# A gated linear attention with a maxout layer: tiles of 128 tokens of one sequence become tiles of 64 tokens of two sequences

## The chip, the cores and the metric

The kernel runs on one core of one Trainium2 chip. The metric is the device time of one execution in microseconds (us). Before the change it is 564.7 us, the median of three runs from 564.04 to 565.69 us.

## What is computed

There are four sequences of 768 tokens and eight heads of 48. Each head keeps a complex 48x48 state that is turned and damped at each token by a gate, takes in an outer product of key and value, and is read by the query. The result, 3072 rows of 384, goes through a maxout layer.

```python
# q, k, v, a_re, a_im: (4, 8, 768, 48); w1, w2, w3: (384, 768); w_out: (768, 384)
mag = np.sqrt(a_re * a_re + a_im * a_im)
scale = np.minimum(mag, 0.999) / (mag + 1e-06)
a_re_n, a_im_n = a_re * scale, a_im * scale
for t in range(768):                       # S_re, S_im start at 0, per batch and head
    new_re = ar * S_re - ai * S_im         # ar, ai: gate of token t, one per row of the state
    new_im = ar * S_im + ai * S_re
    S_re, S_im = new_re + outer(k[t], v[t]), new_im
    y[t] = q[t] @ S_re
x = y.transpose(0, 2, 1, 3).reshape(3072, 384)
out = maximum(maximum(x @ w1, x @ w2), x @ w3) @ w_out
```

## The kernel before

**Tiles and groups.** A tile is 128 tokens of one sequence, that is two chunks of 64, on the 128 partitions. A group is two tiles, called x and y, of two different sequences. There are 12 groups: groups 0 to 5 walk through sequences 0 and 1, groups 6 to 11 through sequences 2 and 3. So the recurrence runs through six groups, and group 6 starts again from an empty state. Inside a tile chunk 1 needs the state that chunk 0 leaves.

**From gates to scores.** For a group, `gates` (L502) works out the logarithm of the gate's size (`Ln`) and its angle in turns (`w`) from `ar` and `ai`. In the word `cs` of `angles` (L583) TensorE sums the angles over the tokens by products with the triangular matrix `upto`: for chunk `ch` of the tile, `lhsT` is all 128 rows of `upto` by the 64 columns of that chunk, so chunk 1 gets the sum over the whole tile. There are four such products per tile (two chunks, even and odd heads), each of 192 columns; a product of 32-bit floats shows as two instructions in the trace. Words `t` (ScalarE) and `nf` (VectorE) take the sum to its fraction of a turn. Word `Cd` (L598) carries it on: two GpSimd-issued DMAs per tile add the last row of `nf` to row 0 of the next group's `ar`, where word `turn` (VectorE) picks it up before the next `cs`. In the last group of a sequence there is no `Cd`. `turns` (L619) sums `Ln` in the same way in the word `sums`, but over chunks of 64 alone, as products of 64 rows by 64 columns in four quarters of the array (eight products per tile). Keys and queries are scaled and turned (`mk`, `mq`, `uk`, `uq`), transposed (`tpk`, `tpq`), weighted by blocks (`factors`, L684: `Q1`, `Q2`, `KB`, `QB`, `QG`), and give the scores `A` and `B`, which VectorE picks into `atm` by masks (`g0` to `g3`).

**State.** `state` (L767): word `kEn` weights the keys, `dk` is the outer products of keys and values for both chunks (four heads only in a sequence's last group), and the words `h0` to `h3` take the state on: `h0`/`h1` decay it and add `dk` of chunk 0, `h2`/`h3` the same for chunk 1, each on 112 partitions by 384 elements on VectorE (the very first `h1` is a copy on ScalarE). Word `y` of `outputs` (L802) adds the scores times the values and the state times the weighted queries `QG`; chunk 0 of a sequence's first tile has no state, so `QG` is made for half of the heads' columns there.

**The layer.** The features of a group are 384 x 256. From `w2 - w1` and `w3 - w1` it takes `U01, U02, U11, U12` products, with the maximum on ScalarE or VectorE (`u..`); `w1` with `w_out` is one product made at the start. The last product is done by seven block products (`P1` to `P7`, sums `S1` to `S4`, joins `r..`, `ox`, `oy`). Group 0 uses plain products instead. The weights come in 12 blocks (`WL0` to `WL11`) whose bits VectorE and ScalarE rearrange at the start (`Wa` to `Wg`).

**Order.** `SCHEDULE` (L21) lists 1903 words, `name` + tile + group (`csx:3`); class `Bound` (L200) makes every engine issue its instructions in that order. `SLOTS` (L125) names the PSUM room for each use, and `OTHER` (L132) the words that go to the second engine they can run on: loads to GpSimd's queue instead of SyncE's (SP), copies and absolute values to VectorE instead of ScalarE, `addw` and `Lnop` to VectorE instead of an adding DMA of GpSimd. Loads (L367 to L392): `Lr`, `Li` bring 128 rows of `a_re`, `a_im` in one transfer; `Lk`, `Lq`, `Lv` take four transfers of 64 rows and four heads each. `D` (L946) writes 128 rows of the result.

Of the kernel before, what the change touches and what calls it, by code (L numbers as in the profile page):

```python
# [26 lines left out]
Wf6:0 mkx:0 CL:0 Wb9:0 tx:0 nfx:0 Wa10:0 Wc9:0 csy:0 ty:0 Wb10:0 afx:0 sumsy:0 sbx:0 sax:0 We9:0 Wc10:0 f2y:0 nfy:0
We10:0 ukx:0 sqr:1 uqx:0 Wf9:0 Eky:0 sqi:1 f1x:0 tpkx:0 Lry:2 Lvx:0 kEnx:0 Eqy:0 f0x:0 Wf10:0 add:1 f2x:0 Kcx:0 tpqx:0
Wa11:0 Wb11:0 Qcx:0 WL1:0 lnL:1 f3y:0 Q2x:0 expw:1 T1:0 Q1x:0 KBx:0 T2:0 Wc11:0 We11:0 t2:0 Wa1:0 t1:0 QBx:0 Lix:2
Ax:0 Wb1:0 g0x:0 Wf11:0 g1x:0 expe:1 Wc1:0 WL2:0 g2x:0 We1:0 relu:1 xor:1 Wf1:0 WL4:0 abs:1 half:1 dkx:0 h1x:0 pw:1  # L30
Liy:2 Wa2:0 Eny:0 g3x:0 Wb2:0 h2x:0 Wc2:0 lne:1 Lnop:1 h3x:0 Lvy:0 We2:0 lnw:1 expL:1 Lkx:1 M0:0 Wg1:0 afy:0 Wa4:0
sby:0 Bx:0 mulw:1 QGx:0 Wf2:0 Lrx:2 mulai:1 sqr:2 Lqy:0 sqi:2 say:0 Wb4:0 mqy:0 b1x:0 Wc4:0 Cdx:0 M1:0 stt:1 uqy:0
We4:0 WL5:0 Cdy:0 Lqx:1 b0x:0 add:2 atan:1 yx:0 lnL:2 Z2:0 tpqy:0 relu:2 Lqy:1 Wf4:0 Qcy:0 mky:0 Lix:4 xx:0 expe:2
Wg2:0 turn:1 uky:0 Wa5:0 M2:0 csy:1 m1:0 tpky:0 Kcy:0 Q1y:0 csx:1 Q2y:0 Wg4:0 xor:2 m0:0 Ay:0 tx:1 kEny:0 dky:0 Wb5:0
expw:2 abs:2 lne:2 QBy:0 h1y:0 g0y:0 nfx:1 g1y:0 g2y:0 g3y:0 U01x:0 WL7:0 Wc5:0 half:2 ty:1 addw:2 u01x:0 KBy:0 Wa7:0
Fx:1 nfy:1 Cdy:1 f1x:1 f0x:1 f3x:1 f2x:1 We5:0 sumsx:1 Cdx:1 QGy:0 Enx:1 By:0 b1y:0 b0y:0 lnw:2 U02x:0 Wf5:0 Ekx:1
expL:2 Eqx:1 Wb7:0 u02x:0 afx:1 h2y:0 Wc7:0 yy:0 xy:0 sbx:1 U11x:0 WL8:0 Wg5:0 mulw:2 Lnop:2 u11x:0 Wa8:0 mulai:2
We7:0 afy:1 stt:2 atan:2 sby:1 U02y:0 sax:1 U01y:0 U11y:0 h3y:0 mkx:1 Liy:3 U12y:0 Wf7:0 turn:2 mqx:1 Wg7:0 u11y:0
sumsy:1 u01y:0 u12y:0 Wb8:0 Eky:1 Z4:0 Fy:1 f2y:1 uqx:1 Eny:1 u02y:0 Wc8:0 Eqy:1 ukx:1 f3y:1 U21y:0 csy:2 Z3:0 We8:0
Wf8:0 Wg8:0 f0y:1 tpqx:1 f1y:1 u21y:0 tpkx:1 ty:2 Qcx:1 U21x:0 u21x:0 Lvy:2 Lvx:2 Kcx:1 Q2x:1 csx:2 U22y:0 kEnx:1  # L40
sumsx:2 nfy:2 h0x:1 Enx:2 tx:2 u22y:0 Lvx:1 mqy:1 Ekx:2 dkx:1 say:1 Lky:1 nfx:2 h1x:1 QBx:1 Lix:3 Oy:0 Lkx:2 sbx:2
afx:2 h2x:1 mky:1 h3x:1 uqy:1 tpqy:1 uky:1 Fx:2 Eqx:2 oy:0 Qcy:1 Q1x:1 KBx:1 tpky:1 QGx:1 f0x:2 Kcy:1 Ax:1 mkx:2 Q1y:1
Q2y:1 Lry:3 g0x:1 Lvy:1 g1x:1 g2x:1 Bx:1 f1x:2 afy:2 f3x:2 U22x:0 u22x:0 say:2 sby:2 g3x:1 Ay:1 b0x:1 sax:2 KBy:1
kEny:1 g0y:1 Lqx:2 mqx:2 sumsy:2 b1x:1 uqx:2 ukx:2 f2x:2 U12x:0 Lrx:3 Eqy:2 sqr:3 Eny:2 yx:1 Eky:2 xx:1 g1y:1 u12x:0
Lky:2 g2y:1 Lqy:2 QBy:1 g3y:1 tpqx:2 h0y:1 Lqx:3 sqi:3 add:3 tpkx:2 mky:2 Qcx:2 lnL:3 dky:1 expw:3 relu:3 expe:3 abs:3
h1y:1 xor:3 Q2x:2 addw:3 h2y:1 Q1x:2 mqy:2 QGy:1 Kcx:2 By:1 b1y:1 Ox:0 uqy:2 uky:2 h3y:1 b0y:1 yy:1 Dy:0 lne:3 Ax:2
xy:1 lnw:3 expL:3 U11:1 U12:1 Lnop:3 ox:0 Lqy:3 g0x:2 Lrx:4 g1x:2 g2x:2 kEnx:2 mulw:3 mulai:3 QGx:2 stt:3 atan:3
half:3 u11:1 Lry:4 g3x:2 h0x:2 tpqy:2 Cdx:2 Qcy:2 tpky:2 Cdy:2 dkx:2 sqr:4 Fy:2 f0y:2 Liy:4 sqi:4 QBx:2 u12:1 h1x:2
U02:1 Liy:5 J3:0 h2x:2 J1:0 f1y:2 h3x:2 KBx:2 U01:1 J2:0 S3:1 Kcy:2 kEny:2 Dx:0 turn:3 add:4 Lky:4 Lix:5 f3y:2 f2y:2
u01:1 Bx:2 Q1y:2 csx:3 tx:3 csy:3 ty:3 h0y:2 u02:1 b0x:2 nfx:3 sumsx:3 Enx:3 afx:3 nfy:3 Lry:5 b1x:2 dky:2 Ekx:3 QBy:2  # L50
Fx:3 P1:1 S1:1 S2:1 J4:0 lnL:4 Lrx:5 f3x:3 P5:1 h1y:2 Eqx:3 expe:4 yx:2 f2x:3 expw:4 h2y:2 Q2y:2 f0x:3 KBy:2 f1x:3
xx:2 xor:4 Ay:2 P7:1 g0y:2 g1y:2 relu:4 S4:1 abs:4 lne:4 addw:4 P6:1 half:4 sbx:3 Lkx:3 mkx:3 Lvx:3 r1:1 Py:1 Px:1
Cdx:3 sby:3 r6:1 r5:1 Lnop:4 mqx:3 sax:3 h0x:3 P4:1 g2y:2 g3y:2 r7:1 lnw:4 P2:1 h3y:2 P3:1 By:2 sumsy:3 expL:4 b0y:2
r57:1 Fy:3 b1y:2 QGy:2 Eny:3 Lvy:3 ox:1 ukx:3 Eqy:3 uqx:3 f0y:3 yy:2 Eky:3 oy:1 sqr:5 Lky:3 xy:2 mulai:4 tpkx:3 tpqx:3
Qcx:3 mulw:4 stt:4 Q2x:3 Kcx:3 atan:4 afy:3 say:3 Liy:6 Q1x:3 QBx:3 f2y:3 mqy:3 mky:3 uky:3 uqy:3 f3y:3 U01:2 QGx:3
f1y:3 U02:2 Lkx:4 Cdy:3 tpqy:3 KBx:3 u01:2 u02:2 Qcy:3 Q1y:3 Lvx:4 tpky:3 Ax:3 sqi:5 Kcy:3 turn:4 add:5 Bx:3 S3:2
g0x:3 g1x:3 g2x:3 Lqy:4 g3x:3 U11:2 kEnx:3 u11:2 csx:4 tx:4 Dx:1 csy:4 Lqx:4 b1x:3 b0x:3 dkx:3 Lry:6 ty:4 xor:5 nfx:4
sumsy:4 h1x:3 sumsx:4 Ekx:4 nfy:4 h2x:3 Eny:4 Lrx:6 afy:4 h3x:3 U12:2 kEny:3 Lix:6 Eqy:4 lnL:5 relu:5 expw:5 mqy:4
Q2y:3 mkx:4 yx:3 Enx:4 u12:2 KBy:3 S1:2 Ay:3 QBy:3 g0y:3 g1y:3 g2y:3 expe:5 abs:5 Eky:4 P7:2 P1:2 Eqx:4 say:4 g3y:3
xx:3 S2:2 Lvy:4 dky:3 afx:4 h0y:3 QGy:3 sax:4 Fx:4 sby:4 sbx:4 h1y:3 lne:5 h2y:3 Px:2 Lvx:5 P6:2 h3y:3 addw:5 Fy:4  # L60
P2:2 half:5 f0y:4 Dy:1 lnw:5 f2y:4 mky:4 ukx:4 P5:2 uky:4 S4:2 Py:2 mqx:4 f3y:4 expL:5 f1y:4 P4:2 uqy:4 f2x:4 f3x:4
By:3 r1:2 f1x:4 P3:2 r6:2 r5:2 b1y:3 b0y:3 f0x:4 yy:3 Lnop:5 xy:3 mulw:5 uqx:4 tpqx:4 r7:2 r57:2 tpqy:4 ox:2 Cdy:4
Qcy:4 h0y:4 U11:3 mulai:5 oy:2 stt:5 Dy:2 sqi:6 atan:5 Qcx:4 Q2y:4 u11:3 Q1y:4 Lky:5 sqr:6 Cdx:4 h0x:4 tpkx:4 tpky:4
Kcy:4 turn:5 QBx:4 Q1x:4 U12:3 add:6 Lry:7 csx:5 xor:6 Q2x:4 tx:5 csy:5 Kcx:4 ty:5 lnL:6 expe:6 lne:6 Ax:4 nfx:5 Lqy:5
Ay:4 nfy:5 kEny:4 relu:6 expw:6 sby:5 u12:3 g0x:4 g1x:4 g2x:4 g3x:4 afx:5 abs:6 Dx:2 sax:5 S3:3 afy:5 QGx:4 g0y:4
g1y:4 U01:3 Liy:7 U02:3 u01:3 Lnop:6 kEnx:4 dkx:4 g2y:4 sumsy:5 g3y:4 sumsx:5 KBx:4 u02:3 Lqx:5 sbx:5 half:6 Lix:7
h1x:4 dky:4 h2x:4 h3x:4 S1:3 P7:3 h1y:4 P5:3 addw:6 S2:3 say:5 Enx:5 h2y:4 Eqx:5 lnw:6 Eqy:5 P1:3 expL:6 mqx:5 mulw:6
Lkx:5 Lvy:5 Eky:5 h3y:4 Bx:4 P6:3 b1x:4 mky:5 uqx:5 KBy:4 QBy:4 b0x:4 S4:3 yx:4 uky:5 Eny:5 Ekx:5 QGy:4 mulai:6 stt:6
r1:3 By:4 xx:4 b1y:4 atan:6 Fx:5 f0x:5 r6:3 mqy:5 r5:3 Py:3 r7:3 turn:6 Lrx:7 b0y:4 f3x:5 Px:3 P3:3 f1x:5 P4:3 f2x:5
P2:3 r57:3 csx:6 uqy:5 sqr:7 mkx:5 ox:3 csy:6 oy:3 ukx:5 sqi:7 ty:6 yy:4 Lky:6 nfy:6 tx:6 xy:4 tpqx:5 Qcx:5 Lkx:6  # L70
nfx:6 Q2x:5 afx:6 tpky:5 add:7 Lqy:6 Kcy:5 lnL:7 tpqy:5 tpkx:5 expw:7 Dy:3 Kcx:5 U11:4 kEnx:5 Q1x:5 Qcy:5 u11:4 expe:7
Fy:5 f0y:5 KBx:5 dkx:5 f1y:5 f2y:5 f3y:5 lne:7 relu:7 h0y:5 Lqx:7 afy:6 Q1y:5 sumsy:6 Eky:6 Q2y:5 abs:7 Ax:5 QBx:5
Dx:3 Eqy:6 g0x:5 h0x:5 g1x:5 h1x:5 Eny:6 xor:7 U01:4 u01:4 U02:4 QGx:5 mqy:6 sax:6 g2x:5 say:6 Lnop:7 Lvy:6 sby:6
g3x:5 mky:6 kEny:5 uqy:6 u02:4 half:7 S3:4 U12:4 u12:4 Bx:5 b1x:5 Ay:5 g0y:5 Lix:8 dky:5 addw:7 b0x:5 sumsx:6 Enx:6
Eqx:6 Ekx:6 g1y:5 lnw:7 S1:4 P1:4 expL:7 P7:4 Liy:8 Lvx:6 h1y:5 KBy:5 QBy:5 By:5 g2y:5 S2:4 yx:5 g3y:5 b0y:5 mulw:7
Lrx:8 tpqy:6 r1:4 P6:4 sbx:6 Qcy:6 mulai:7 b1y:5 QGy:5 P5:4 Lry:8 stt:7 Lqx:6 mqx:6 Px:4 Py:4 r6:4 Fy:6 uqx:6 xx:5
# [966 lines left out]
```

## Time and profile before

| | us |
|---|---|
| median of 3 runs | 564.7 |
| lowest, highest run | 564.04, 565.69 |
| profiled execution, device time | 566.65 |
| its span, first to last instruction | 564.9 |
| TensorE matmul busy | 526.3 |
| VectorE busy | 491.1 |
| ScalarE busy | 384.6 |
| GpSimd busy | 160.4 |

PE is TensorE's matmuls, PEld its weight loads, DVE VectorE, ACT ScalarE, POOL GpSimd, SP SyncE, which only issues DMAs; `SPq` is its queue. In rows of instructions `out<-in` are the program's names, then partitions x elements and how often; after the bar come the busy time in us and the mean of one in ns, and after the second bar the engine's idle time just before them with its cause. All instructions pass a helper, so they share line L209 and are told apart by their tiles. In rows of windows each engine's busy time in the stretch is followed by its number of instructions; then come the granted TensorE clock, the mean busy share of the 16 DMA engines and GB/s.

### The profile page before, as it was taken

How to read it: one execution, taken by the hardware profiler on the slowest of the kernel's cores; microseconds unless marked ns; L12 is line 12 of the kernel's file. 1: busy time of each engine (PE TensorE's matmuls, PEld its weight loads, DVE VectorE, ACT ScalarE, POOL GpSimd, SP SyncE). 2: the span in 40 equal slices, each digit the busy share in tenths (PEclk: the TensorE clock that was granted, in tenths of full speed). 3: DMA queues.
4: the chain of work that ended last, by engine and by line, in shares of the span. 5: the costliest groups of instructions: out<-in, count | busy, mean ns of one | idle time of the engine just before them, and what ended most of it. 6: DMA issues, size and time to landing. Idle time of an engine off the chain costs nothing.

```text
span 564.9 us, 22784 instructions
## 1 busy us (share of the span) xinstructions
PE 526.3 (93%) x10086; PEld 450.5 (80%) x10086; DVE 491.1 (87%) x776; ACT 384.6 (68%) x664; POOL 160.4 (28%) x250
## 2 busy tenths in 40 slices
...
GB/s 231 267 226 121 210 160 80 86 84 102 59 97 115 47 60 98 89 62 139 17 67 97 58 68 114 48 50 108 30 46 24 79 71 32 3 31 2 2 15 42
DMA packets 106851, 47.13 MB, mean 83 GB/s; under 512 B 93568, under 2 KB 98176, under 8 KB 106752
## 3 DMA queue, kind: packets, MB, share of 16 engines
...
## 4 chain that ended last, share of the span: by engine, by line
PE 76%; ACT 11%; DVE 7%; issue 3%; DMA 2%; SPq 0%; DVEq 0%; ACTq 0%; POOLq 0%
PE up L209 32%; PE op L209 20%; PE y L209 5%; PE A L209 4%; PE dk L209 3%; PE tp L209 3%; PE cs L209 3%; DVE xhx L209 2%; PE sums L209 2%; ACT f L209 2%; ACT L209 1%; PE B L209 1%; PE F L209 1%; ACT L L209 1%; ACT atm L209 1%
## 5 line engine op out<-in xcount | busy, mean ns | idle before, releaser
L209 PE MATMUL up<-xhx,w 128*128 128x256 f32 x792 | 177.7, 382 | 0.4 <-ACT f L209 0.4
L209 PEld LDWEIGHTS up<-xhx,w 128*128 128x128 f32 x792 | 148.5, 190 | 21.4 <-ACT f L209 0.5
L209 ACT ACT_TABLE_LOAD x53 | 68.0, 1283 | 1.6 <-PEq L1027 0.8
L209 POOL DMA_DIRECT2D k<-in_k_dram x48 | 31.9, 771 | 80.3 <-DVE uk L209 66.9
L209 PE MATMUL op<-wo,xhx 128*128 128x192 f32 (+1 forms) x220 | 49.5, 364 | 0.0
L209 POOL DMA_DIRECT2D ar<-nf x40 | 37.6, 1403 | 36.8 <-DVE ar L209 27.5
L209 DVE TENSOR_TENSOR Q<-Q,f 112x1024 f32<-112x1024 f32 (+1 forms) x48 | 45.0, 951 | 2.8 <-ACT Q L209 1.4
L209 POOL DMA_DIRECT2D vb<-in_v_dram x56 | 41.2, 1044 | 20.0 <-PE y L209 18.3
L209 ACT COPY atm<-B 32x128 f32<-32x128 f32 x96 | 24.5, 255 | 30.1 <-DVE atm L209 21.9
L209 PE MATMUL y<-atm,vb 128*32 128x64 f32 x1152 | 39.2, 221 | 2.8 <-POOL vb L209 1.8
L209 PEld LDWEIGHTS op<-wo,xhx 128*128 128x128 f32 x220 | 36.5, 190 | 3.8 <-DVE strassen L209 0.3
L209 PEld LDWEIGHTS y<-atm,vb 128*32 128x32 f32 x1152 | 32.7, 109 | 8.3 <-POOL vb L209 2.3
L209 PE MATMUL y<-QG,g 112*32 112x64 f32 x1408 | 38.1, 219 | 0.2
L209 ACT ACTIVATE f<-F 48x232 f32<-48x232 f32 x96 | 34.4, 358 | 5.5 <-PE F L209 4.2
L209 DVE TENSOR_TENSOR ot<-ot,op 128x192 f32<-128x192 f32 (+1 forms) x66 | 27.0, 416 | 10.8 <-PE op L209 7.5
L209 PEld LDWEIGHTS y<-QG,g 112*32 112x32 f32 x1408 | 34.8, 109 | 0.3 <-issue 0.3
L209 POOL DMA_DIRECT2D Ln<-e x9 | 12.7, 1408 | 78.6 <-ACT e L209 59.6
L209 DVE TENSOR_TENSOR xhx<-xhx,up 128x768 f32<-128x768 f32 x22 | 20.9, 951 | 15.5 <-PE up L209 15.2
L209 PE MATMUL op<-w,strassen 128*128 128x192 f32 x176 | 32.8, 332 | 1.3 <-DVE atm L209 1.2
L209 POOL DMA_DIRECT2D q<-in_q_dram x40 | 26.6, 805 | 23.3 <-DVE uq L209 23.3
L209 PE MATMUL op<-wo,strassen 128*128 128x192 f32 x176 | 32.5, 328 | 0.0
L209 DVE COPY_PREDICATED atm<-masko,A 128x256 f32<-128x256 uint8 x72 | 31.2, 434 | 1.4
...
## 6 DMA issues: line engine op xcount, KB each, us to landing
ai<-in_a_im_dram SPq DMA_DIRECT2D x24, 192.0 KB, 5.0
ar<-in_a_re_dram SPq DMA_DIRECT2D x24, 192.0 KB, 4.0
out_dram<-ot SPq DMA_DIRECT2D x24, 192.0 KB, 2.3
...
q<-in_q_dram SPq DMA_DIRECT2D x56, 48.0 KB, 2.9
vb<-in_v_dram POOLq DMA_DIRECT2D x56, 48.0 KB, 4.2
...
```

Source lines behind the costliest of these rows:

```text
L209: ins = f(*a, **kw)
```

## The change

A tile becomes 64 tokens of each of two sequences: tile x holds sequences 0 and 1, tile y sequences 2 and 3, with one of the two on each "chunk" place. All 12 groups walk down the 768 tokens together, so the recurrence runs through 12 groups, and no tile depends on itself. The sums of angles become products of 64 by 64 rows and columns, put in two banks. The carry `Cd` goes to rows 0 and 64 and is done after every group but the last. The state is taken on once per tile, in two words of 768 elements. Gates and results move in transfers of 64 rows (twice as many, half the size); keys, queries and values in transfers of 64 rows and eight (sequence, head) pairs (half as many, twice the size). The second halves of the gates of group 0, and of the last results, are issued by ScalarE. `SCHEDULE` (1859 words), `SLOTS` and `OTHER` are written anew; the words `h2`, `h3`, `QG:0` and `dk:11` and `h0:11`, `h1:11` are gone, `Cd:5` and `h0:6` are new, and `kEn:11` stays.

```diff
-Liy:0 sqi1:0 Lry:0 sqr1:0 add1:0 lnL1:0 Lky:0 Lrx:0 Lix:0 Zg:0 sqr0:0 expe1:0 sqi0:0 lne1:0 xor1:0 WL0:0 WL3:0 expw1:0
...
+Lrx:0 sqr0:0 Zg:0 Lix:0 sqi0:0 add0:0 Lry:0 Liy:0 Zf:0 WL0:0 WL3:0 sqr1:0 lnL0:0 xor0:0 WL6:0 sqi1:0 xor1:0 expe0:0
+expw0:0 Lqx:0 lne0:0 relu0:0 add1:0 lnL1:0 Lnop0:0 abs0:0 half0:0 Wa0:0 WL9:0 expw1:0 expe1:0 Fx:0 relu1:0 lne1:0
...
+S2:11 P2:11 Dx:10 P6:11 S4:11 P3:11 r6:11 r5:11 ox:11 P7:11 Py:11 Dx:11 kEny:11 P4:11 r7:11 r57:11 oy:11 Dy:11
...
-    NG = B // C * NS
+    NG = S // L64
...
+    def rows(a, g, b):
+        return a[b, :, g * L64:(g + 1) * L64, :].rearrange("h t d -> t h d")
+    def half(a, g, c, j):
+        a = a.rearrange("(c b) h t d -> c (b h) t d", c=C)
+        return a[c, j::2, g * L64:(g + 1) * L64, :].rearrange("h t d -> t h d")
     def load_a(g, c, nm, src):
-        sp.dma_start(out=t[:, c], in_=rows(src, g, c))
+        for ch in range(2 if g > 0 else 1):
+            sp.dma_start(out=t[ch * L64:(ch + 1) * L64, c], in_=rows(src, g, 2 * c + ch))
     def load_kq(g, c, nm, src):
         for j in range(2):
-            for ch in range(2):
-                (pool if other() else sp).dma_start(out=t[j * L64:(j + 1) * L64, ch], in_=halves(src, g, c, j)[:, ch])
+            (pool if other() else sp).dma_start(out=t[j * L64:(j + 1) * L64].rearrange("p c i d -> p (c i) d"),
+                                                in_=half(src, g, c, j))
...
-            ps = T["cs", x] = banks("cs", DM)
-            for ch in range(2):
-                for j in range(2):
-                    dst, m = ps[j * L64:(j + 1) * L64, ch * HC:(ch + 1) * HC], slice(ch * L64, (ch + 1) * L64)
-                    mm(out=dst, lhsT=upto[:, m], rhs=every(T["w", g][:, c * DM:(c + 1) * DM], j), start=True, stop=True)
+            ps = T["cs", x] = banks("cs")[:, :, 0:HC]
+            for j in range(2):
+                for ch in range(2):
+                    r = slice(ch * L64, (ch + 1) * L64)
+                    mm(out=ps[j * L64:(j + 1) * L64, ch], lhsT=upto[r, r],
+                       rhs=every(T["w", g][r, c * DM:(c + 1) * DM], j), start=True, stop=True)
...
         elif name == "Cd":
-            if (g + 1) % NS > 0:
-                    pool.dma_start(out=every(t[:, c * DM:(c + 1) * DM], j), accum_op=OP.add,
-                                   in_=T["nf", x][last - 1:last, HC:].rearrange("p (i d) -> p i d", d=D))
+                to = bass.AP(to.tensor, to.offset, [[pitch * L64, 2]] + [list(d) for d in to.ap][1:])
+                pool.dma_start(out=to, accum_op=OP.add,
+                               in_=T["nf", x][last - 1:last].rearrange("p (c i d) -> p c i d", c=2, d=D))
...
-            g = 0 if x // C % NS > 0 else H
-            times(rows8(QG[0:DD, g:]), rows8(T["Q", x][0:DD, 2 * g:, 0:32]), CG, 8, g)
+            times(rows8(QG[0:DD]), rows8(T["Q", x][0:DD, :, 0:32]), CG, 8)
...
-            for n in range(H if s < NS - 1 else 4):
+            for n in range(H):
...
+        elif name in ("h0", "h1"):
+            new = both_chunks(gs[(x + C) % 4][0:DD])
+            if name == "h0":
+                F = T["F", x][0:DD, :, :, CD:CD + 1]
+                dve.tensor_tensor(out=new, in0=both_chunks(gs[x % 4][0:DD]), in1=F.to_broadcast([DD, H, 2, D]), op=OP.mult)
                 return True
+            dk = T["dk", x][0:DD, :, 0:DM].rearrange("p j (n d) -> p n j d", d=D)
+            if x < C:
+                act.copy(out=new, in_=dk)
             else:
+                dve.tensor_tensor(out=new, in0=new, in1=dk, op=OP.add)
...
-            sp.dma_start(out=out[t0:t0 + P, :], in_=T["ot", x])
+            for ch in range(2):
+                t0 = (2 * c + ch) * S + g * L64
+                queue = act if ch and g == NG - 1 else sp
+                queue.dma_start(out=out[t0:t0 + L64, :], in_=T["ot", x][ch * L64:(ch + 1) * L64])
...
     constants_early()
+    for c in range(C):
+        for nm, src in (("ar", a_re), ("ai", a_im)):
+            t = once((nm, 0), lambda: ld2.tile([P, C, H, D], FP, tag=nm, name=nm))
+            act.dma_start(out=t[L64:, c], in_=rows(src, 0, 2 * c + 1))
     T["set"] = SETS[AF.Ln]
     act.preload_act_table_set(T["set"])
```

More of the change, by code (lines that the diff above doesn't have):

```diff
@@ L27 @@
[L27 to L76, printed above, removed]
```

216 lines of the change are left out of this document (122 added, 94 removed).

## The prediction

> **What bounds the kernel now.** I read the page's busy shares and the shares of the chain that ended last, then windows of time, then the groups of instructions by shape.
>
> ```profile
> span 564.9 us, 22784 instructions
> PE 526.3 (93%) x10086; PEld 450.5 (80%) x10086; DVE 491.1 (87%) x776; ACT 384.6 (68%) x664; POOL 160.4 (28%) x250
> ...
> PE 76%; ACT 11%; DVE 7%; issue 3%; DMA 2%; SPq 0%; DVEq 0%; ACTq 0%; POOLq 0%
> ```
>
> The two windows below (after the stretch and its length: busy time of PE, PEld, DVE, ACT, POOL, then the clock, the DMA share and GB/s) split the run at 90 us, where PE becomes full.
>
> ```profile
> 0.00:90.00 90.00, 60.75 (x944) 43.85 (x946) 81.75 (x138) 76.83 (x134) 48.70 (x88) 0.91 0.85 196
> 90.00:565.00 475.00, 465.51 (x9144) 406.61 (x9144) 409.33 (x639) 307.72 (x531) 111.69 (x163) 1.00 0.31 62
> ```
>
> From 90 us on PE is busy 465.5 of 475 us: only 9.5 us are left between its bursts, and what shortens PE's work there shortens the run. DVE has 409.3 us in that stretch: it has 66 us to spare. Before 90 us PE is idle for 29 us, and these windows say why:
>
> ```profile
> 0.00:10.00 10.00, 0.00 (x0) 0.00 (x0) 5.66 (x20) 7.00 (x16) 7.88 (x31) 1.00 0.79 202
> 10.00:20.00 10.00, 6.08 (x56) 3.13 (x56) 9.79 (x16) 7.22 (x14) 9.48 (x16) 1.00 1.13 268
> 20.00:30.00 10.00, 5.94 (x70) 3.82 (x70) 9.96 (x20) 9.51 (x16) 5.12 (x10) 0.66 1.03 273
> 30.00:40.00 10.00, 6.21 (x101) 5.13 (x105) 9.85 (x14) 9.82 (x17) 0.00 (x0) 0.66 0.73 218
> ```
>
> From 10 us on DVE is busy 9.8 to 10 of each 10 us, from 20 us ACT nearly so; the weights' bits and the gates go through them. In the first 10 us they wait for data. So: the start is DVE's and ACT's, the rest is PE's.
>
> **The change part by part.**
>
> *The sums of angles* (`cs`). The rows of the PE groups by shape, then pieces of the chain of work in order of time (start, length, what); in the last two, two tiles follow each other without a wait between:
>
> ```profile
> L209 PE MATMUL cs<-w,upto 128*64 128x192 f32 x192 | 20.2, 351 | 3.9 <-DVE w L209 1.7 <-ACT f L209 1.2 <-ACT E L209 0.5
> ...
> L209 PE MATMUL sums<-Ln,mid 64*64 64x192 f32 x192 | 13.8, 347 | 1.2 <-DVE Ln L209 0.6 <-DVE nf L209 0.5
> ```
>
> ```profile
> 64.11 0.87 PE cs L209 x8
> ...
> 89.11 0.87 PE cs L209 x8
> ...
> 411.61 1.45 PE cs L209 x16
> ```
>
> ```profile
> 479.91 1.46 PE sums L209 x32
> ```
>
> A `cs` of two tiles is 16 instructions in 1.45 us, 91 ns each; `sums` of two tiles is 32 instructions in 1.46 us, 46 ns each, at the same 192 columns and about the same duration of one (351 and 347 ns). The difference is how many run side by side: `cs` takes all 128 rows and half the columns of the array, so two at a time; `sums` takes a quarter, so four. After the change `cs` has the very shape of `sums`, its order (the two chunks next to each other), and a bank of PSUM for each chunk as `sums` has. Its 8 instructions per tile should take 8 x 46 ns = 0.365 us where they took 0.725: 0.36 us less per tile. The `cs` of group 1 ends with the piece at 64 us, group 2 begins at 89: groups 2 to 11 (20 tiles) lie on the bound, and 20 x 0.36 = 7.2 us come off it. The four tiles before that (1.4 us) lie where DVE and ACT set the pace, and I count them at nothing.
>
> The Trainium skill weighs against the full factor. Its page "TensorE: Matmul & The Clock Gate", Part 3 (measured speedup against the span model), gives four row tiles a gain of 3.07, not 4; taken as the yield of all four quarters here, `cs` would cost about 0.47 us, an estimate by that page, and 20 tiles would save 5.1 us. The rows of `sums` show the whole factor of two against `cs`.
>
> *The state.* DVE and ACT rows:
>
> ```profile
> L209 DVE TENSOR_TENSOR uk<-uk,En 128x768 f32<-128x768 f32 x24 | 22.8, 949 | 0.0
> ...
> L209 DVE TENSOR_TENSOR g<-g,f 112x384 f32<-112x384 f32 x40 | 22.1, 552 | 1.1 <-ACT f L209 0.7
> L209 DVE TENSOR_TENSOR g<-g,dk 112x384 f32<-112x384 f32 x40 | 21.9, 548 | 3.3 <-PE dk L209 2.8
> ...
> L209 DVE TENSOR_TENSOR QG<-Q,f 112x512 f32<-112x512 f32 x4 | 2.7, 680 | 0.0
> ```
>
> 80 DVE instructions of 384 elements (44.0 us) become 40 of 768 (10 groups x 2 tiles x 2; 0.95 us each like any 768 here): 38.0 us, 6.0 less. In group 0 `h2`, `h3` (4 x 0.55) and `QG` (2 x 0.68) go: 3.6 us of DVE in the start. The wait for `dk` inside a tile (2.8 us over the run, DVE's) goes; what is late next is `dk` of the group before, some 40 us earlier. PE's work for `dk` and `y` is the same in number: 22 tiles x 8 heads against 20 x 8 + 4 x 4, and 44 chunks with a state in both. `kEn:11` is left without a reader: 2 x 0.95 us of DVE in the tail, where DVE is busy 18 of 50 us:
>
> ```profile
> 515.00:565.00 50.00, 46.30 (x533) 41.26 (x531) 18.32 (x31) 2.95 (x8) 0.00 (x0) 0.99 0.05 17
> ```
>
> *The carry.* `Cd` gives 44 GpSimd DMAs for 40:
>
> ```profile
> L209 POOL DMA_DIRECT2D ar<-nf x40 | 37.6, 1403 | 36.8 <-DVE ar L209 27.5 <-issue 6.3 <-DVE nf L209 2.9
> ```
>
> ```profile
> ar<-nf POOLq DMA_DIRECT2D x40, 0.8 KB, 3.9
> ```
>
> New is that `turn:6` (DVE) waits for group 5. Queued behind it on DVE are `uky:5`, `add:7`, `h0x:5`, and PE's `tpky:5` waits for the first. A late `Cd` costs at most its issue and landing, 2 x 1.4 + 3.9 = 6.7 us, once; between `Cdx:5` and `turn:6` the list has some 10 us of DVE work (`mulai`, `mulw`, `stt`, `QGx`, `h1x` and others), so I take 0.
>
> *Transfers.* By the lists SP issues 226 DMAs for 228, GpSimd 137 for 204; ACT gets 6. A row of GpSimd's:
>
> ```profile
> L209 POOL DMA_DIRECT2D k<-in_k_dram x48 | 31.9, 771 | 80.3 <-DVE uk L209 66.9
> ```
>
> A transfer twice as large may cost GpSimd between 0.77 us and twice that; in neither case is an engine that is busy 160 of 565 us the bound. From 90 us on the DMA share is 0.31, so I cost all later transfers at nothing: the cover is PE's full list, and the price if it goes is one landing (2.9 to 5.0 us) per late load. At the start:
>
> ```profile
> 0.81 0.44 SPq L209 DMA_DIRECT2D ai<-in_a_im_dram  x1
> ...
> 1.31 1.41 SPq L209 DMA_DIRECT2D ar<-in_a_re_dram  x2
> ...
> 2.10 0.51 ACT L209 ACTIVATE uk<-biases 128x128 f32<-128x128 f32 x2
> 2.51 0.49 ACT L209 ACTIVATE uq<-biases 128x128 f32<-128x128 f32 x2
> ...
> 3.73 0.52 ACT L209 ACTIVATE L<-ai 128x384 f32<-128x384 f32 x1 [0.73 <-DMA ai<-in_a_im_dram]
> ...
> 5.42 0.56 DVE L209 CUSTOM_DVE_ANT_0 L<-L,e 128x384 f32<-128x384 f32 x1 [2.43 <-ACT e L209]
> 5.99 1.09 DVE L209 MEMSET g<- 128x256 f32 x4
> ...
> 7.52 0.52 ACT L209 ACTIVATE L<-ai 128x384 f32<-128x384 f32 x1 [0.15 <-DMA ai<-in_a_im_dram]
> ```
>
> ```profile
> L209 ACT ACT_TABLE_LOAD x53 | 68.0, 1283 | 1.6 <-PEq L1027 0.8
> ```
>
> After the change ACT starts at 0.8 us with four DMA issues (0.4 to 0.7 us each by SP's rows, 2.3 us), then loads its table (1.28) and clears four tiles (0.9), so its first square starts near 5.3 us instead of 3.73. But ACT is idle 3 of its first 10 us now, 0.8 of them ahead of all, and the clearing of `g` (1.09 us of DVE) now comes ahead of the first `add`. I take 1 us lost, bounds 0 and 2.5.
>
> *The lists.* The moves in `OTHER` take 7 instructions of 0.95 us from DVE (five `addw`, `Lnop`, `Wg` to GpSimd, two `u` to ACT) and give it two more `Kc`:
>
> ```profile
> L209 DVE COPY K<-tp 112x1024 f32<-112x1024 f32 x5 | 6.1, 1219 | 0.9 <-PE tp L209 0.9
> ```
>
> That is 4.2 us less on DVE. ACT switches its table 56 times for 52 by the lists, 4 x 1.28 = 5.1 us more of 307.7 busy in 475. Both engines have room for it after 90 us. How well the new order packs, no row of before shows. The nearest is the 9.5 us of PE gaps after 90 us: bounds 6 better and 6 worse, I take 0, since the same engines release the same kinds of work. Of the 3.6 us of DVE relief in group 0 I take 2, since ACT, as full as DVE from 20 us, gets none.
>
> *The end.* PE is full to the last products; each `D` is two halves on two queues instead of one transfer. I take 0.
>
> **The sum**: -7.2 (`cs`) - 2.0 (start, DVE) + 1.0 (start, ACT) = -8.2 us against the span of 564.9 us; the profiled execution took 566.65 with what lies around it, and the change moves nothing there. From the median of the runs, 564.7, that gives 556.5 us.
>
> **The rivals.** *The new order packs worse*: PE's gaps grow by 4 us, three or four waits like these two of PE after 90 us:
>
> ```profile
> PE cs L209 <- ACT f L209: 1.2, 1, 1.2
> PE op L209 <- DVE atm L209: 1.2, 1, 1.2
> ```
>
> That gives 560.5. For it: ACT, which releases half of such waits, carries 5 us more of table loads, and the carry now runs through 12 groups. *It packs better*: the whole 3.6 us of DVE relief and 2 to 3 us of gaps go: 552.5. For it: DVE has 10 us less in all, and a state that is ready a group ahead. *The quarters do not run side by side*: `cs` stays at 0.725 us, and only the start's 1 us is won: 563.7. Against it stand the 46 ns of `sums`.
>
> *Slower, by the 64-row loads at the start.* The mechanism: a load of 64 rows moves at half the rate of one of 128, and the two halves don't make up for it. The four gate loads of 128 rows (768 KB) took from 0.81 us to 7.5 us, 6.7 us; as eight halves they would take 13.4, and DVE, which has no work of group 0 without them, starts 6.7 us later; group 1's gates come after them in the stretch where the DMA share is 1.03 to 1.13, another 6.7. That gives 556.5 + 13.4 = 570, and it ends slower from a loss of 8.2 us on. Against it: keys of 64 rows land well today,
>
> ```profile
> ai<-in_a_im_dram SPq DMA_DIRECT2D x24, 192.0 KB, 5.0
> ...
> k<-in_k_dram SPq DMA_DIRECT2D x48, 48.0 KB, 2.7
> ```
>
> 48 KB in 2.7 us against 192 KB in 5.0, and the two halves go out on two queues at once. The Trainium skill states this rule: the page "SBUF — State Buffer", section "Door 1: The DMA port swizzle", says that 64 rows reach no more DMA ports than 32, and that two DMAs to the two halves gain little. No row of before shows two such halves in flight at once.
>
> **How the numbers follow.** Forecast (554.5 to 558.5) 0.47; packs worse 0.18 (a fifth of it past 563); packs better 0.19; quarters not side by side 0.08; slower start 0.08. About 0.3% (1.7 us) is what a measurement of this kernel can tell from no change, so same is 563.0 to 566.4. Faster: 0.47 + 0.19 + 0.14 + 0.03 = 0.83; same: 0.05 + 0.04 = 0.09; slower 0.08. The range, 550.0 to 563.0, takes in the bounds of the packing beside the forecast (6 us each way, rounded out) and leaves out the last two cases and the worst of the first.
>
> **What would show it.** `cs` of two tiles at 16 instructions in about 0.75 us, its row near 10 us instead of 20.2; PE's busy time near 518; `g` rows as 20 + 20 of 768 at 0.95; gaps of PE after 90 us still near 9.5; the first square near 5.3 us and DVE full from 10 us on. It is wrong if `cs` keeps 91 ns per instruction, if DVE's first 10 us hold less than 4 us of work, or if PE's gaps after 90 us exceed 14 us.

## The result

The changed kernel takes 558.31 us (median of 6 runs, 556.94 to 559.99) against 564.56 (6 runs, 563.89 to 565.69): a ratio of 0.9891, 95% interval 0.9871 to 0.9911. That is 6.25 us less; the prediction said 8.2 less, 556.5. The profiled execution of the changed kernel took 559.11 us, 0.8 above its median, that of the kernel before 566.65, 2.1 above: the two profiled spans differ by 7.5 us.

### The profile page after: what moved, and what is told of

Read it like the earlier page. It is cut to its first block, busy times and chain, and to the rows that moved or that the text cites. A ratio compares the mean times of both kernels' runs of the same rounds, so it can differ in the third digit from the quotient of the medians.

```text
span 557.4 us, 22649 instructions
## 1 busy us (share of the span) xinstructions
PE 517.6 (93%) x10086; PEld 445.9 (80%) x10086; DVE 483.3 (87%) x726; ACT 390.3 (70%) x669; POOL 127.0 (23%) x183
## 4 chain that ended last, share of the span: by engine, by line
PE 71%; ACT 9%; DVE 2%; issue 1%; SPq 1%; DMA 1%; ACTq 0%
PE up L205 30%; PE op L205 18%; PE y L205 6%; PE A L205 4%; PE dk L205 4%; PE tp L205 3%; ACT L205 3%; PE sums L205 2%; ACT CS L205 1%; PE cs L205 1%; PE B L205 1%; PE F L205 1%; ACT f L205 1%; SPq L205 1%; ACT L L205 1%
## 5 line engine op out<-in xcount | busy, mean ns | idle before, releaser
L205 POOL DMA_DIRECT2D ar<-nf x44 | 41.9, 1421 | 54.4 <-DVE ar L205 49.5
L205 DVE TENSOR_TENSOR Q<-Q,f 112x512 f32<-112x512 f32 (+1 forms) x48 | 45.0, 951 | 0.9 <-ACT Q L205 0.9
L205 POOL DMA_DIRECT2D w<-L x9 | 8.6, 955 | 126.0 <-ACT L L205 45.8
L205 PE MATMUL A<-Q,K 112*32 112x80 f32 x1536 | 31.4, 238 | 1.5 <-DVE Q L205 1.5
L205 ACT ACTIVATE xhx<-up 128x768 f32<-128x768 f32 x19 | 15.4, 809 | 23.2 <-PE up L205 23.2
L205 PEld LDWEIGHTS A<-Q,K 112*32 112x32 f32 x1536 | 28.3, 112 | 4.1 <-ACT K L205 2.1
```

Of the source, the lines that this page charges most:

```text
L205: ins = f(*a, **kw)
```

## The profile after

First the page's head and its chain of work:

```profile
span 557.4 us, 22649 instructions
PE 517.6 (93%) x10086; PEld 445.9 (80%) x10086; DVE 483.3 (87%) x726; ACT 390.3 (70%) x669; POOL 127.0 (23%) x183
...
PE 71%; ACT 9%; DVE 2%; issue 1%; SPq 1%; DMA 1%; ACTq 0%
```

PE's busy time fell by 8.7 us with as many instructions, DVE's by 7.8 with 50 fewer, ACT's rose by 5.7. Then the two windows that the prediction was built on:

```profile
0.00:90.00 90.00, 59.18 (x874) 42.86 (x874) 78.47 (x131) 74.97 (x133) 41.27 (x76) 0.83 0.88 199
90.00:557.40 467.40, 458.42 (x9220) 403.03 (x9212) 404.79 (x596) 315.36 (x537) 85.78 (x107) 1.00 0.35 67
```

PE's work behind 90 us is 458.42 us, 7.1 less than the 465.51 of before, and its gaps there are 467.40 - 458.42 = 9.0 us, where they were 9.4. That makes the 7.5 us. Ahead of 90 us nothing was won: PE did 1.6 us less there, which is the share of its four early tiles in the shorter work (24 tiles lost 8.7), so at 90 us the program is about as far as it was. The start also ran at a lower TensorE clock in this execution, 0.83 granted over the first 90 us against 0.91 in that of the kernel before.

Where the 7 us are, the groups by shape show:

```profile
L205 PE MATMUL cs<-w,upto 64*64 64x192 f32 x192 | 12.1, 352 | 2.0 <-ACT Q L205 0.9 <-ACT hT L205 0.5 <-DVE w L205 0.4
...
L205 DVE TENSOR_TENSOR g<-g,f 112x768 f32<-112x768 f32 x20 | 19.0, 952 | 0.5 <-ACT f L205 0.5
L205 DVE TENSOR_TENSOR g<-g,dk 112x768 f32<-112x768 f32 x20 | 19.0, 952 | 1.2 <-PE dk L205 0.8
```

192 instructions of `cs` fill 12.1 us instead of 20.2 while the mean of one has stayed (352 ns for 351): four run side by side where two did. In the chain of work 14 of the 16 instructions of a group's two tiles take 0.67 us, 48 ns each; in other groups all 16 take 0.65 to 0.81 us, 41 to 51 ns each:

```profile
140.64 0.67 PE cs L205 x14
141.31 0.65 PE sums L205 x16
```

Last the start, as a timeline (start, length, engine, what; in brackets the wait ahead of it and what ended it) and PE's waits in the first 90 us (us in all, times, longest):

```profile
0.80 0.73 ACTq L205 DMA_DIRECT2D ar<-in_a_re_dram  x1
0.81 0.76 SPq L205 DMA_DIRECT2D ar<-in_a_re_dram  x1
...
2.92 0.66 ACTq L205 DMA_DIRECT2D ai<-in_a_im_dram  x1
3.00 1.09 DVE L205 MEMSET g<- 128x256 f32 x4
3.61 1.28 ACT L205 ACT_TABLE_LOAD   x1 [3.61 <-issue]
5.72 0.51 ACT L205 ACTIVATE e<-ar 128x384 f32<-128x384 f32 x1
...
7.82 0.51 ACT L205 ACTIVATE L<-ai 128x384 f32<-128x384 f32 x1
```

```profile
PE F L205 <- DVE Ln L205: 10.8, 1, 10.8
PE tp L205 <- DVE uq L205: 3.6, 1, 3.6
PE up L205 <- DMA w<-w: 3.2, 1, 3.2
```

ACT's first square starts at 5.72 us and the last of the four at 7.82 us, and none waits for a DMA: the eight halves of 64 rows were there when the engines came. The third of PE's waits is new.

```profile
63.88 1.31 POOL L205 DMA_DIRECT2D w<-w  x1 [0.91 <-DVE w L205]
...
68.36 1.60 PE L205 MATMUL up<-xT,w 128*128 128x128 f32 x12
...
73.20 2.90 PE L205 MATMUL up<-xT,w 128*128 128x128 f32 x12 [3.24 <-DMA w<-w]
...
76.62 2.83 PE L205 MATMUL up<-xT,w 128*128 128x128 f32 x12
```

GpSimd issues an adding DMA for block 4 of the first projection's weights (`Wg4:0`) at 63.88 us, and PE waits for it until 73.20, in the very stretch in which the DMA share is 1.10:

```profile
70.00:80.00 10.00, 6.80 (x100) 6.42 (x104) 8.84 (x16) 4.08 (x11) 4.75 (x6) 0.66 1.10 216
```

The block was formed by such a DMA in the kernel before too, but issued at 60.02 us, and the product that reads it stood third among the first `up` products; in the new order it stands second. The wait isn't all that it costs here: the granted clock of that stretch is 0.66, and the two dozen products behind the wait take 2.90 and 2.83 us where the dozen ahead of it took 1.60.

## The experiments

The **PE theory** (A in most expectations) is the prediction's own: behind 90 us PE sets the pace, so the shorter `cs` is nearly the whole gain, and DVE's and ACT's work there is covered. Its first rival: the gain is **DVE's** (the state in whole instructions, less work in group 0), and PE only follows. After e2 came the **list theory** (L): behind 90 us PE, DVE and ACT are tied together by the lists, and relief of one of them pays only in lists made for it. All ratios are against the kernel before, run beside it on the same chip; e1 to e4, the f runs with e5 and e6, and the g runs were on three different chips.

| run | median us | ratio (95%) | span us |
|---|---|---|---|
| e1_cs_128_rows | 566.27 | 1.0014 (0.9996 to 1.0033) | 564.6 |
| e2_before_cs_64 | 565.49 | 0.9997 (0.9974 to 1.0020) | 564.0 |
| e3_wg4_dve | 556.44 | 0.9838 (0.9812 to 0.9864) | 555.1 |
| e4_act_two | 560.93 | 0.9916 (0.9890 to 0.9942) | 559.0 |
| f1_before_no_h2 | 563.87 | 0.9976 (0.9956 to 0.9995) | 561.0 |
| f2_before_both | 563.18 | 0.9971 (0.9949 to 0.9993) | 559.7 |
| e5_qg0_back | 556.47 | 0.9846 (0.9820 to 0.9871) | 555.3 |
| e6_state_halves | 560.18 | 0.9902 (0.9874 to 0.9930) | 557.1 |
| g1_old_lists | 582.25 | 1.0330 (1.0299 to 1.0361) | 580.3 |
| g2_dve_more | 565.08 | 1.0004 (0.9979 to 1.0029) | 562.8 |
| g3_better | 555.15 | 0.9835 (0.9812 to 0.9858) | 553.7 |
| g4_after_again | 558.42 | 0.9893 (0.9867 to 0.9920) | 558.2 |

### e1: the changed kernel with its angle sums over 128 rows

```
-            for j in range(2):
-                for ch in range(2):
+            for ch in range(2):
+                for j in range(2):
...
-                    mm(out=ps[j * L64:(j + 1) * L64, ch], lhsT=upto[r, r],
-                       rhs=every(T["w", g][r, c * DM:(c + 1) * DM], j), start=True, stop=True)
+                    mm(out=ps[j * L64:(j + 1) * L64, ch], lhsT=upto[:, r],
+                       rhs=every(T["w", g][:, c * DM:(c + 1) * DM], j), start=True, stop=True)
```

(and one clearing of `upto`'s corner block on GpSimd, which keeps the other sequence out of the sum.)

> The changed kernel with one thing undone: the four angle products of a tile take all 128 rows again (the triangular matrix has its corner block set to zero, so the sums are the same), two at a time in the array; lists, transfers and state stay changed. Theory A, the time came from four products side by side on a full PE: the cs row goes back from 12.1 to about 20 us busy, two tiles of cs from about 0.75 to 1.45 us, and the time rises by 20 x 0.36 = 7.2 us, from 558.3 to about 565.5. Theory B, the time came from the new lists, loads and state, and PE would have waited elsewhere anyway: the time stays within 2 us of 558.3.

The whole gain is gone: 566.27 us. Its `cs` row, and the window behind 90 us:

```profile
L205 PE MATMUL cs<-w,upto 128*64 128x192 f32 x192 | 20.3, 351 | 1.7 <-ACT Q L205 0.5 <-ACT hT L205 0.5 <-ACT vb L205 0.4
```

```profile
90.00:600.00 510.00, 465.19 (x9212) 406.85 (x9210) 404.40 (x594) 314.65 (x537) 85.59 (x107) 1.00 0.31 61
```

PE's work is 465.19 us again, its gaps 564.6 - 90 - 465.2 = 9.4. Set side by side, the same instruction of DVE or ACT starts 0.8 us earlier in e1 than in the changed kernel at 110 us, 1.0 later at 185, 3.2 at 285, 5.1 at 335, 7.2 at 485: the loss comes in evenly, tile by tile. In the new lists each 0.36 us that is put back on PE counts in full, as the PE theory says, and the gain isn't DVE's alone. That taking as much off PE would count in any order doesn't follow; e2 tries it.

### e2: the kernel before with the 64x64 angle sums alone

```
-            ps = T["cs", x] = banks("cs", DM)
...
+            ps = T["cs", x] = banks("cs")[:, :, 0:HC]
...
+                    r = slice(ch * L64, (ch + 1) * L64)
+                    mm(out=ps[j * L64:(j + 1) * L64, ch], lhsT=upto[r, r],
+                       rhs=every(T["w", g][r, c * DM:(c + 1) * DM], j), start=True, stop=True)
```

> The kernel before with one thing of the change alone: its angle products are 64 by 64 in two banks, with t and nf reading both banks. This leaves out a part of the computation: chunk 1 of a tile does not get the angle sum of chunk 0. Theory A: 7.2 us less, 564.6 to about 557.4, as much as the whole change brought or a little more. Theory B: less than 2 us, 562.6 or above.

The PE theory expected nearly the whole gain of the changed kernel; measured is 565.49, no change. The products are as short as in the changed kernel, and PE's work behind 90 us did fall, from 465.5 to 460.5 us:

```profile
L209 PE MATMUL cs<-w,upto 64*64 64x192 f32 x192 | 12.7, 359 | 3.8 <-DVE w L209 1.5 <-ACT f L209 1.3 <-ACT E L209 0.5
```

```profile
90.00:600.00 510.00, 460.53 (x9130) 400.75 (x9128) 408.50 (x639) 307.29 (x530) 111.62 (x163) 1.00 0.29 58
```

But the gaps rose from 9.4 to 564.0 - 90 - 460.5 = 13.5: of 5 us won, 4 went to waiting. The PE theory in its plain form falls here. What holds PE back shows when the middle of the run is cut into stretches of 100 us, first of the kernel before, then of e2:

```profile
150.00:250.00 100.00, 98.95 (x2070) 86.65 (x2072) 95.45 (x151) 79.68 (x136) 28.75 (x41) 1.00 0.39 74
250.00:350.00 100.00, 98.61 (x1950) 86.17 (x1939) 92.39 (x143) 76.85 (x129) 37.76 (x55) 1.00 0.44 84
350.00:450.00 100.00, 98.07 (x2103) 86.73 (x2102) 90.19 (x144) 70.08 (x124) 18.43 (x27) 1.00 0.28 55
```

```profile
150.00:250.00 100.00, 97.85 (x2109) 85.45 (x2109) 95.10 (x151) 79.70 (x137) 29.22 (x42) 1.00 0.39 76
250.00:350.00 100.00, 97.05 (x1897) 84.39 (x1893) 92.34 (x143) 76.11 (x127) 37.50 (x55) 1.00 0.43 84
350.00:450.00 100.00, 97.26 (x2105) 86.15 (x2104) 90.47 (x144) 70.40 (x124) 18.44 (x27) 1.00 0.27 54
```

DVE does 95, 92 and 90 us of work in 100, in both kernels alike, and PE loses what it had won. The chain of e2 went from 76% PE to

```profile
PE 57%; issue 13%; ACT 12%; DVE 9%; POOL 6%; DMA 2%; SPq 0%; DVEq 0%; ACTq 0%; POOLq 0%
```

### f1 and f2: less work for DVE in the kernel before, and both together

f1 is the kernel before without 14 of its decays of the state (`h2`, the one of chunk 1, for both tiles of groups 2 to 4 and 7 to 10, 7.7 us of DVE); f2 is e2 and f1 in one.

```
-            if c > 0 and s == NS - 1 or s + c + i == 0:
+            if c > 0 and s == NS - 1 or s + c + i == 0 or c > 0 and i == 0 and s > 0 and x >= 2 * C:
```

> The kernel before without 14 of its VectorE instructions: the decay of the state by chunk 1 (h2) is left out in groups 2 to 4 and 7 to 10, 14 x 0.55 = 7.7 us of VectorE; nothing else differs. After the angle products alone brought nothing in the kernel before, three theories: A (PE alone sets the pace; then the missing gain is odd): 0. D (PE and VectorE's list set the pace together, relief on one alone buys little): 0 to 2 us less, 562.7 to 564.7. V (VectorE alone sets the pace): 7 us less, 557.5.

> The kernel before with the 64 by 64 angle products (chunk 1 without chunk 0's sum) and without the 14 decays, so 7 us less on PE and 7.7 us less on VectorE. D: both reliefs together bring 5 to 7 us, 557.7 to 559.7, though each alone brings less than 2. L (the order is packed so closely that a shorter instruction only lengthens the next wait, until the lists are made anew): less than 2.5 us, 562 or above. V: as f1.

f1 gave 0.24%, f2 0.29%: the relief of PE and that of DVE together are worth 2.1 us by the medians. f1 alone would fit theory D as well as L; f2 decides against D, which expected 5 to 7 us. Against the kernel before, instruction by instruction, f1 gains 1.5 us between 110 and 485 us, and f2 1.7; most of what else the spans differ by arises between 60 and 85 us, ahead of the omitted decays, where the granted clock differs from one execution to the next: from 70 to 80 us it is 0.87 in the trace of the kernel before and 1.00 in f1's and f2's. f2's window:

```profile
90.00:600.00 510.00, 457.19 (x9092) 398.74 (x9092) 398.38 (x622) 304.77 (x526) 110.91 (x161) 1.00 0.28 57
```

457.2 us of PE work and 398.4 of DVE's are both less than the changed kernel has there (458.4 and 404.8), and yet the gaps are 559.7 - 90 - 457.2 = 12.5 us. So it isn't enough to call DVE a second bound beside PE, to be relieved along with it: in the old order, these two reliefs together mostly leave holes.

### g1: the change with the lists of before

The changed kernel's code with the old `SCHEDULE`, `SLOTS` and `OTHER`. From `SCHEDULE` go the entries that are without work now, `Cd` of group 5 comes in, and so do the two decays `h0` of group 6, ahead of their sums; `SLOTS` loses the turns of the entries that are gone:

```
-... h2x:0 ... h3x:0 ... QGx:0 ... QGy:0 ... h2y:10 h3y:10 ... h0x:11 h0y:11 ... dky:11 dkx:11 ... h1x:11 h1y:11
+... half:6 Cdx:5 Cdy:5 Lix:7 ... KBx:6 h0x:6 h1x:6 ... uqx:7 h0y:6 h1y:6
```

> The changed kernel (tiles of two sequences, 64 by 64 angle products, whole-tile state, new transfers) with the lists of the kernel before: SCHEDULE, SLOTS and OTHER as they were, less the words that have no work any more (h2, h3, QG:0, dk:11, h:11), plus the two carries of group 5 behind half:6 and h0:6 ahead of h1:6. Theory L (shorter work pays only where the lists are made for it): 563 to 566, like the kernel before. Theory G (the geometry's shorter work pays by itself): 557 to 560, like the changed kernel.

582.25 us, 24 us above the same code with the new lists and 18 above the kernel before: far outside both expectations, since the list theory had expected the time of the kernel before. Its PE work behind 90 us is 463.7 us, and the gaps are 580.3 - 90 - 463.7 = 26.6; they are spread through the run:

```profile
90.00:600.00 510.00, 463.72 (x9171) 403.20 (x9169) 406.57 (x601) 304.94 (x526) 85.16 (x107) 0.99 0.28 57
...
150.00:250.00 100.00, 93.04 (x1953) 81.03 (x1952) 86.91 (x129) 73.67 (x125) 25.40 (x31) 0.98 0.37 73
250.00:350.00 100.00, 94.20 (x1950) 81.86 (x1950) 92.96 (x138) 75.88 (x128) 22.49 (x30) 1.00 0.35 71
```

In 150 to 250 us neither PE (93 of 100) nor DVE (87) is full. PE's waits behind 90 us name no single culprit; the two largest are 4.7 and 3.3 us, and ACT's waits show one thing that stands behind the first:

```profile
PE y L205 <- ACT atm L205: 4.7, 4, 3.7
PE dk L205 <- issue: 3.3, 3, 1.7
```

```profile
ACT L L205 <- DMA w<-L: 14.4, 4, 6.2
```

This row is the wait for the DMA by which GpSimd adds to the gates' angles (`addw`). ACT waits 14.4 us for it here, 8.7 in the kernel before and 0.4 in the changed kernel. The longest of these waits ends at 240.95 us, and the longest of PE's waits for `atm`, 3.7 us, follows from it: the copy of `atm` that PE waits for stands behind it in ACT's list. How much of the loss runs this way isn't told apart.

So the lists belong to the change: with the old ones in this form it is 3.3% slower than the kernel before. A caution: g1 is the old order with the smallest edits that the new code needs; how much of the 18 us is due to where the new entries were put isn't told apart.

### g2: more DVE work in the changed kernel

A second, needless `QG` for tile x in groups 2 to 10, nine instructions of 1.22 us.

```
-... QGx:2 Kcy:2 ... QGx:3 Eny:4 ...
+... QGx:2 QGx:2 Kcy:2 ... QGx:3 QGx:3 Eny:4 ...
```

> The changed kernel with nine more VectorE instructions on the dense stretch: QG of tile x is made twice in groups 2 to 10 (9 x 1.22 = 11.0 us of VectorE), the second copy is the one that is used. If VectorE has room there, as the prediction had it (405 us busy in 467), the time rises by less than 2 us. If VectorE's list is as tight as PE's, it rises by 5 to 11 us.

565.08 us, 6.7 more than the control g4 on the same chip: 11 us of DVE by durations (10.2 by its busy time in the whole run) cost 6.7.

```profile
90.00:600.00 510.00, 458.23 (x9191) 401.98 (x9190) 412.84 (x602) 313.30 (x536) 85.53 (x107) 1.00 0.31 61
```

PE has the work of the changed kernel (458.2), and its gaps grew to 562.8 - 90 - 458.2 = 14.6. The prediction had called DVE's 66 free microseconds behind 90 us room to spare. In the kernel before 41 of them lie behind 450 us:

```profile
450.00:600.00 150.00, 111.30 (x1811) 99.21 (x1809) 73.72 (x119) 36.17 (x68) 10.69 (x16) 0.99 0.07 19
```

From 90 to 450 us DVE is free for 24 of 360. A theory that names PE alone, or DVE alone, is refuted by e1 and g2 together: in the new order 6.8 us more of PE's work behind 90 us cost 7.2 us of span, and 11 us more of DVE's cost 6.7 of the median.

### e6: the state in halves again

```
-                dve.tensor_tensor(out=new, in0=new, in1=dk, op=OP.add)
+                for n in (slice(0, 4), slice(4, 8)):
+                    dve.tensor_tensor(out=new[:, n], in0=new[:, n], in1=dk[:, n], op=OP.add)
```

(and the decay likewise.)

> The changed kernel with the state taken on in halves, 80 VectorE instructions of 384 in the place of 40 of 768: 6.0 us more on VectorE by durations, lists and the rest unchanged. A (the changed kernel is PE's alone): 0 to 1 us more, up to 559.3. D (VectorE sets the pace with PE): 2.5 to 6 us more, 561 to 564.

560.18 us, about 1.9 above the changed kernel, with intervals that overlap, and between the two theories; by the starts of the same instructions, 0.9 us between 110 and 485 us. The dose was smaller than I had thought:

```profile
90.00:600.00 510.00, 457.52 (x9196) 402.52 (x9194) 405.32 (x634) 313.66 (x536) 85.56 (x107) 1.00 0.31 61
```

38 more DVE instructions behind 90 us than the changed kernel, and DVE is busy 405.3 us for 404.8; over the whole run, which counts the same work in both, it is 484.9 for 483.3, 1.6 more. By durations, 80 instructions of 0.55 us against 40 of 0.95 make 6 us; in busy time two halves back to back take little longer than one whole. So the run says little on the theories, and much on that term.

### e3, e4, e5: the start

e3 forms `Wg4` on DVE instead of by GpSimd's adding DMA (one more entry in `OTHER`); e4 lets ACT issue two of the four early gate loads and SP the other two; e5 puts the two `QG` of group 0 back, 2.4 us of DVE.

```
-Lqx:0 abs0:0 Lkx:0 Lqy:1 Wg8:0 ...
+Lqx:0 abs0:0 Lkx:0 Lqy:1 Wg4:0 Wg8:0 ...
```

```
-    for c in range(C):
-        for nm, src in (("ar", a_re), ("ai", a_im)):
...
-            act.dma_start(out=t[L64:, c], in_=rows(src, 0, 2 * c + 1))
+    for nm, src in (("ar", a_re), ("ai", a_im)):
...
+        act.dma_start(out=t[L64:, 0], in_=rows(src, 0, 1))
```

```
-... b0x:0 yx:0 ... b0y:0 yy:0 ...
+... b0x:0 QGx:0 yx:0 ... b0y:0 QGy:0 yy:0 ...
```

> The changed kernel with weight block 4 added by VectorE (0.95 us) instead of by an adding DMA of GpSimd. In the changed profile PE waits 3.2 us for such a DMA at 70 to 73 us, and the DMA took 9.4 us to land. Theory A, the start lost the DVE relief to this wait: the wait goes, 558.3 less 1 to 2.5 us, 556 to 557.3. Theory C, the start is still DVE's and a wait of PE there costs nothing: 0 to 1 us more, 558.3 to 559.3.

> The changed kernel with only two gate loads of group 0 issued by ScalarE (tile x's second halves) and the other two by SP behind its own. In the changed profile ScalarE issues four in 2.8 us and its first square starts at 5.72 us, against 3.73 us before. Theory A, these issues delay the start: the first square starts near 4.4 us and the time falls by about 1 us, to 557.3. Theory C, what the start needs is the weights' bits, whose loads SP now issues 1.3 us later: no gain, 558.3 to 559.6.

> The changed kernel with two more VectorE instructions in group 0: QG is made for both tiles as in the other groups (2 x 1.22 us), and nobody reads it. If the start is VectorE's (the prediction), the time rises by 1.5 to 2.4 us, to about 560.3; if the start waits for PE, ScalarE and late weights instead (Theory C), by less than 0.7.

e3 gives 556.44 us, and its gain arises where it should: the same instructions start 1.8 us later than in the changed kernel at 61 us, 3.1 earlier at 85, and stay 2.3 to 2.9 earlier to the end. By its median e3 lies 1.9 us below the changed kernel, by the ratios 3.0. (The block's DMA took 9.2 us to land; the 9.4 of the expectation is that of the next one, issued at 70.20 us.)

e4 gives 560.93, above both expectations. Two issues fewer ahead of ACT's table did bring the first square to 4.36 us, as expected; but the second then waits for its load, and a later one 1.09 us more:

```profile
4.36 0.51 ACT L205 ACTIVATE e<-ar 128x384 f32<-128x384 f32 x1
5.64 0.52 ACT L205 ACTIVATE L<-ai 128x384 f32<-128x384 f32 x1 [0.77 <-DMA ai<-in_a_im_dram]
```

e5 was expected to cost something and came out at 556.47, below both expectations. Up to 75 us its instructions do start later than the changed kernel's, by 1.7 us at 68 and 2.1 at 75. Then they start 2.4 us earlier at 85, and 2.0 to 2.1 earlier from 95 to 185. In between lies the late DMA: PE's wait for it is half as long, and the products behind it run at a granted clock of 1.00 from 70 to 80 us, where it was 0.66:

```profile
73.58 1.58 PE L205 MATMUL up<-xT,w 128*128 128x128 f32 x12 [1.53 <-DMA w<-w]
75.47 1.61 PE L205 MATMUL up<-xT,w 128*128 128x128 f32 x12
```

So in these traces the wait for the DMA swallowed 1.7 of the 2.1 us of delay, and the faster products, 2.5 us for two dozen, put e5 ahead. The other runs fit that: the mean granted clock of a whole run was 0.977 to 0.985 in e5's six, 0.972 to 0.979 in the changed kernel's six. What lowers the clock there is open: of seven traces with this wait, the products behind it take 2.7 to 2.9 us in five (waits of 2.6 to 3.2 us) and 1.6 in two (e5, and g2 with a wait of 3.36).

### g3 and g4: a version that beats both, and the control

g3 is the changed kernel with `Wg4` on DVE and without the two `kEn:11` that nothing reads. g4 is the changed kernel unaltered, on the same chip.

```
-... b0x:11 kEnx:11 u12:10 ... Dx:11 kEny:11 P4:11 ...
+... b0x:11 u12:10 ... Dx:11 P4:11 ...
-Lqx:0 abs0:0 Lkx:0 Lqy:1 Wg8:0 ...
+Lqx:0 abs0:0 Lkx:0 Lqy:1 Wg4:0 Wg8:0 ...
```

> The changed kernel with weight block 4 added on VectorE and without the two kEn of group 11 that nobody reads. If the gain of the first was one of the kernel and not of the chip it ran on, 1.5 to 3 us below the changed kernel run beside it; kEn by itself 0 to 0.3. If the spread of the start between runs made it, within 1 us of it.

> The changed kernel once more, unaltered, on the chip of the three others, as their measure: 556.5 to 559.5. Its start, compared with its first profile instruction by instruction, tells how far the same kernel's start moves between two executions: up to 2 us if the start is what spreads the runs, less than 0.5 if not.

g3 takes 555.15 us (554.77 to 555.45), the control 558.42 (556.99 to 559.95): 3.3 us, with intervals that don't meet. PE's three longest waits of the start have no DMA among them any more:

```profile
PE F L205 <- DVE Ln L205: 10.8, 1, 10.8
PE tp L205 <- DVE uq L205: 3.6, 1, 3.6
PE F L205 <- ACT E L205: 2.7, 1, 2.7
```

Of 4.5 us that the trace of g3 is ahead of g4's at 485 us, 3.2 are there at 85: the late DMA is the larger part. In g4's trace it cost the wait of 3.23 us and one dozen products at 2.90 us instead of 1.60; in g3's neither shows. Two executions of one kernel (g4's trace and the changed kernel's) differ by up to 0.85 us at the same points.

## Why the prediction was right, and where it wasn't

**The angle sums** (-7.2): right in mechanism and size. PE's work behind 90 us fell by 7.1, and e1 takes the whole gain back. The sentence of the forecast that rested on it, that what shortens PE's work there shortens the run, held here only in the new order: e2 has the same short products in the old order and gains nothing.

**"It has 66 us to spare"**: wrong. The mean over 475 us hid that DVE is busy 95 of 100 us from 150 to 250 and 92 from 250 to 350; g2 paid 6.7 us for 11 us of DVE. The forecast survived, most likely, since the change takes work from DVE too (4.5 us behind 90 us) and puts it in an order made for it.

**The lists** (0, bounds 6 either way): the value was right for these lists, 9.0 us of gaps for 9.4. No row stood behind that 0, so that it came out was luck as far as the prediction goes. And they are no side matter: with the old ones the same code stands 24 us higher. Loads, products and state instructions are the change's body, and between these two sets of lists they decide its sign. I had named the right rival (the order packs worse) and priced it at 4 us, from two waits of PE; a bad order makes many small waits on several engines at once, those for GpSimd's adding DMAs among them.

**The start** (-2.0 and +1.0): a net gain of 1.0 was counted, and at 90 us it is 0. This is the step that failed. ACT's first square came at 5.72 us (forecast near 5.3); whether that cost the 1 us isn't shown, since e4's earlier square only met a later load. The relief of DVE seems to have come as far as 68 us: the first dozen `up` products start 1.4 us earlier than in the kernel before (68.36 for 69.75, though not all the same words stand ahead of them). What the sum left out is the wait behind it: `Wg4`, whose adding DMA the new order issues later and needs sooner, 3.2 us of wait and 2.5 us of slower products in this trace. In e5 this wait swallows most of what DVE's added work had delayed; e3 and g3 remove the wait and gain 2 to 3.3 us. With it gone the kernel stands 1.4 us below my 556.5 (g3, which also drops `kEn:11`).

**The state** (6.0 us of DVE, which I had not put in the sum): too large. It was reckoned from durations, and consecutive instructions overlap; e6 shows 1.6 us of busy time over the run. DVE has 4.5 us less behind 90 us, not the 10 of the state and the lists together.

**The rivals.** Quarters not side by side: fallen, 48 ns an instruction. In the chain two tiles' `cs` took 91 ns an instruction before (16 in 1.45 us) and take 48 now (14 in 0.67), a factor of 1.9; in the whole row, slow early tiles included, 20.2 us became 12.1, not the 10 that was forecast. Between e1 and the changed kernel PE's work behind 90 us differs by 465.2 - 458.4 = 6.8 us. The 5.1 us that the prediction had estimated by the 3.07 for four row tiles, which the Trainium skill's page "TensorE: Matmul & The Clock Gate" gives in Part 3, are too low for this case. Slower by 64-row loads at the start: fallen; the eight halves were there by 7.82 us, where the rival had put 13.4. The Trainium skill's page "SBUF — State Buffer", section "Can I just issue two DMAs to hit both halves?", says that two such loads at once gain little over one; no run here compares the two alone, and ACT's own issues and table load covered what the loads took. The two packing rivals: neither came; but g1 shows what the first would have looked like.

**What stays open**: what the larger transfers of keys, queries and values are worth by themselves was not tried; the only wait of PE's or DVE's in the trace that ends at one of them is 0.4 us of DVE's. What lowers the clock behind the wait for `Wg4` in some executions is open, and so is how much of g1's loss another placing of its few new entries would take back.
